# Threshold attention with a squared-ReLU MLP on one core: the second MLP layer by Strassen's seven products, in chunks of 256 tokens

## The chip, the cores and the metric

The kernel runs on one NeuronCore of a Trainium2 chip. The metric is the device time of one execution, in microseconds (us); the time of a kernel is the median of its runs. Engines are called as in the profile: PE (TensorE; PEld is its weight loading), DVE (VectorE), ACT (ScalarE), POOL (GpSimd), SP (SyncE, whose queue issues nearly all DMAs here).

## The reference

All arrays are float32 (the weights come from the host as 8-byte words, which the kernel reads as double precision and rounds itself).

```python
# q, k, v: (8, 8, 576, 64)   w_in: (512, 2048)   w_out: (2048, 512)
scores = q @ k.T / sqrt(64)
thresh = max(scores, -1) - tau            # tau = 0.02
scores = where(scores >= thresh, scores, -1e9)
attn = exp(scores - max(scores, -1)); attn /= attn.sum(-1) + 1e-9
x = (attn @ v)                            # to (8 * 576, 512): tokens x heads * dims
out = relu(x @ w_in) ** 2 @ w_out         # (4608, 512)
```

## The kernel before

**Attention.** Heads are taken in pairs, four pairs (`HP`) to a batch element, 32 pairs in all. A *visit* is a pair with a list of query blocks, and a *step* is one block of 128 queries (the fifth block, of 64 queries, takes both heads in one tile). There are 160 steps. In a step:

- `scores` (L168): PE computes q k^T of both heads into two PSUM tiles `s0`, `s1` (2 banks each, one copy); DVE takes the maxima (L186) and the thresholds (L187).
- `exponents` (L191): ACT computes exp (L196) into `w`.
- `threshold` (L199): DVE compares the scores with the threshold, multiplies and sums (L208). Only then are the score tiles free for the next step.
- `divide` (L215): POOL multiplies by the reciprocal sums (L220).
- The weights are then transposed to `wT`. The first eleven visits do this on PE two steps later (`turn`, L223, through PSUM and ACT); from step 35 on (`by_dma`) DVE transposes blocks of 32 (`turn_blocks`, L258, one step later) and SP's DMAs place them (`place_blocks`, 16 or 8 DMAs).
- `mix` (L281): PE multiplies by v (L291), ACT copies the result into `xT`, the MLP's input with the channels on the partitions (L295 to L300).

`load_qk`, `load_v` and `prep` (L155) bring in q, k, v of the next visit; `prep` transposes q and k on DVE (L160) into `qT`, `kT`, two buffers of each.

**Weights.** 32 pieces of 128 x 512 (16 of `w_in`, 16 of `w_out`) are loaded by DMA four pieces ahead and rounded by `round_weights` (L101): ACT twice, DVE three times (L116 to L119), POOL twice (L121, L123), in two buffers shared with `turn_blocks`. They are spread over the first 34 steps.

**MLP.** Tokens go in 12 chunks of 384. `mlp_in` (L306): for each of 16 blocks of 128 hidden units, 4 matmuls of 384 columns into `h`; ACT applies ReLU (L317), POOL squares (L318) into `g`. `mlp_out` (L322): for each 128 tokens, 16 matmuls of 512 columns with `g` as the stationary operand, into `o`; ACT copies `o` out (L332) and SP stores it.

**Order.** The order on every engine is written out by the loop at the end; nothing is reordered afterwards. Four times a step `fill` takes matmul pieces of the MLP from a list (`waiting`) and puts them between attention's work. `rate` says how many microseconds' worth a step gets, so that the list lasts until the next chunk's tokens are complete (`chunk_at`). The first four pairs are visited twice, first with three blocks and then with two, so that chunk 0 is complete in step 14; chunk 1 follows in step 40. Until weights are rounded (`out_from`), only the first layer of chunk 0 is spread. After the last step everything left is emitted at once.

Of the kernel before, what the change touches and what calls it, by code (L numbers as in the profile page):

```python
# [19 lines left out]
def kernel(  # L20
# [14 lines left out]
    P = 128  # L35
# [7 lines left out]
    TCH = 384  # L43
    NCH = n_tokens // TCH
    SCALE = 0.125
    assert (H % 2, D, REST, NBLK, d_model) == (0, 64, 64, 4, H * D)
    assert n_tokens == B * S and (2 * S) % TCH == 0 and SCALE * SCALE * D == 1.0
# [13 lines left out]
    w_out_sb = const.tile([P, NFT, d_model], FP32, name="w_out_sb")  # L61
# [5 lines left out]
    qmid = [const.tile([P, P], FP32, name=f"qmid{i}") for i in range(2)]  # L67
    for i in range(2):
        nc.gpsimd.memset(vs[i], 0.0)
        nc.gpsimd.memset(qmid[i], 0.0)  # L70

    WP = 512
    n_in = d_ff // WP * NMC
    n_pieces = n_in + NFT * d_model // WP
    area = {}

    def weight_piece(i):

        if i < n_in:
            f, c = divmod(i, NMC)
            cols = slice(f * WP, (f + 1) * WP)
            return moe_w_in[c * P:(c + 1) * P, cols], w_in_sb[:, c, cols]
        i -= n_in
        return moe_w_out[i * P:(i + 1) * P, :], w_out_sb[:, i, :]

    RAW = 4

    def weight_area(i):  # L90
        if not area:
            area["a"] = pool.tile([P, NMC, 2 * S], FP32, tag="xT", name="area").rearrange("p c s -> p (c s)")
        at = (i % RAW) * 2 * WP
        return area["a"][:, at:at + 2 * WP]

    def load_weights(i):
        nc.sync.dma_start(out=weight_area(i).bitcast(mybir.dt.int64), in_=weight_piece(i)[0])

    rounding = {}

    def round_weights(i, stage):  # L101
# [6 lines left out]
        if stage == 0:  # L108
            rounding[i] = pool.tile([P, 3, WP], FP32, tag="wb", name="cv")
        t, e, d = (rounding[i][:, x, :] for x in range(3))  # L110
# [9 lines left out]
        elif stage == 2:  # L120
            nc.gpsimd.tensor_tensor(out=d, in0=d, in1=e, op=ALU.mult)  # L121
        else:
            nc.gpsimd.tensor_tensor(out=weight_piece(i)[1], in0=t, in1=d, op=ALU.add)  # L123

    loaded, ready = {}, {}

    def load_qk(n):
# [4 lines left out]
        tiles = []  # L132
        for name, t in (("ql", q), ("kl", k)):
            x = pool.tile([P, S // 32, 32], FP32, tag=name, name=name)
            for m in range(4):
# [3 lines left out]
                nc.sync.dma_start(out=to[:, last:, :], in_=src[:, 0:S // 32 - last, :])  # L139
                if last:  # L140
                    nc.sync.dma_start(out=to[:, 0:last, :], in_=src[:, S // 32 - last:, :])
            tiles.append(x)
        loaded[n] = tiles
# [11 lines left out]
    def prep(n, part):  # L155

        if part == 0:
            ready[n] = [pool.tile([P, S], FP32, tag="qT", name="qT"), pool.tile([P, S], FP32, tag="kT", name="kT")]
        qT, kT = ready[n]
        nc.vector.transpose((qT, kT)[part], loaded[n][part].rearrange("p c d -> p (c d)"))  # L160
        if part == 0 and NBLK in visits[n][1]:
            for u in range(2):
                rows = slice(u * D, (u + 1) * D)
                nc.gpsimd.tensor_copy(out=qmid[n % 2][rows, u * D:(u + 1) * D], in_=qT[rows, NBLK * P:S])
# [3 lines left out]
    def scores(vis, i):  # L168

        qT, kT = ready[vis]  # L170
# [5 lines left out]
        for half, u in halves:  # L176
            if i < NBLK:
                rows, lhsT = slice(u * D, (u + 1) * D), qT[u * D:(u + 1) * D, i * P:(i + 1) * P]
            else:
                rows, lhsT = slice(0, P), qmid[vis % 2]  # L180
# [7 lines left out]
        w = pool.tile([P, n, S], FP32, tag="w", name="w", bufs=3)  # L188
# [33 lines left out]

    def turn(vis, i, part):  # L223

        w = weights[vis, i][0]
        ps = psum.tile([P, 4, P], FP32, tag="mm" if early() and part == 1 else "tx", name="w_ps", bufs=2)
# [19 lines left out]
    KB = S // 32  # L246
    blocks = {}

    def turn_blocks(vis, i):
# [4 lines left out]
        if not two or i % 2 == 0:  # L254
            blocks[vis, i // 2] = pool.tile([P, 2 * KB, 2, 32] if two else [P, KB, 1, 32], FP32, tag="wb", name="wb")
# [22 lines left out]
    xTs = {}  # L278
    xTs = {}

    def mix(n, cols):  # L281

        b, pr = divmod(visits[n][0], HP)
        if b // 2 not in xTs:
            xTs[b // 2] = pool.tile([P, NMC, 2 * S], FP32, tag="xT", name="xT")
        nq = cols.stop - cols.start
        ps = psum.tile([P, TCH], FP32, tag="tx", name="x_ps", bufs=2)
# [241 lines left out]
```

## Time and profile before

| | |
|---|---|
| median of 3 runs | 1491.63 us (1490.35 to 1493.38) |
| the profiled execution: time, span | 1489.97 us, 1488.2 us |
| mean granted clock of TensorE | 0.987 |
| PE, PEld busy | 1434.4 us (96%), 765.9 us (51%) |
| DVE, POOL, ACT busy | 801.2 us (54%), 527.2 us (35%), 443.6 us (30%) |
| second layer `o` (L328), first layer `h` (L313) on the chain that ended last | 34%, 32% |
| `s` (L181), `x_ps` (L291) on it | 12%, 10% |

How to read the profile's lines below. A line of groups gives source line, engine, operation, output <- inputs by the program's names, shapes, x count, then busy us and the mean ns of one, then idle time of the engine ahead of it and what ended it (`<-`). A timeline line gives start us, length us, engine, line, operation, and x how many were merged; in brackets the idle time ahead. A line of waits reads "engine line <- what it waited for: us in total, times, longest". A line of a stretch gives `from:to length`, then each engine's busy time with its instructions, then the granted clock, the DMA share and GB/s. A matmul's own length includes its way through the array; in a run of matmuls the spacing of starts is what each costs.

### The profile page before, as it was taken

The numbers are of one execution on the slowest core, as the hardware profiler recorded it, in microseconds if no ns is written. First come the engines' busy times: TensorE is split into PE (matmuls) and PEld (weight loads), VectorE is DVE, ScalarE is ACT, GpSimd is POOL, SyncE is SP. The second block draws the span as 40 slices with busy tenths as digits, with TensorE's granted clock in tenths as the row PEclk, the third lists the DMA queues.
The fourth block names the chain that finished last, engine by engine and source line by source line (L and its number), as shares of the span: only waits on it lengthen the run. The fifth ranks groups of instructions, "written<-read, shape, count | busy, mean of one in ns | idle before, by whom it ended". The sixth has DMA issues, their size and how long they took to land.

```text
span 1488.2 us, 18872 instructions
## 1 busy us (share of the span) xinstructions
PE 1434.4 (96%) x5876; PEld 765.9 (51%) x5876; DVE 801.2 (54%) x1738; ACT 443.6 (30%) x956; POOL 527.2 (35%) x779
## 2 busy tenths in 40 slices
PE   4888889999999999999999999999999999999998
PEld 3665555554455455455455455455455455455453
DVE  5888996655555555555555555555555555510000
ACT  3665564232132232232232122232232222211010
POOL 3567775243143143243233234234134134121020
PEclk9889999999999999999999999999999999999999
DMA  6456530344454554544445544544455444430000
GB/s 150 98 131 136 123 98 22 68 87 86 92 94 83 106 97 80 98 90 82 90 95 92 103 89 81 92 93 84 89 106 92 87 93 86 84 63 7 15 0 22
DMA packets 532547, 125.74 MB, mean 84 GB/s; under 512 B 523744, under 2 KB 523744, under 8 KB 532448
## 3 DMA queue, kind: packets, MB, share of 16 engines
q1 hardware_dynamic: 532416, 124.53, 43.7%
q8 instruction: 48, 0.79, 0.2%
q14 instruction: 51, 0.42, 0.1%
q0 software_dynamic: 32, 0.00, 0.0%
HBM read 48.63 MB, written 9.44 MB: 39 GB/s over the span
## 4 chain that ended last, share of the span: by engine, by line
PE 89%; DVE 7%; SPq 1%; issue 1%; POOL 1%; ACT 0%; DMA 0%; DVEq 0%; ACTq 0%
PE o L328 34%; PE h L313 32%; PE s L181 12%; PE x_ps L291 10%; DVE st L186 2%; DVE cv L117 1%; DVE w L208 1%; PE w_ps L231 1%; SPq L139 1%; DVE cv L116 1%; DVE cv L119 0%; DVE st L187 0%; DVE kT L160 0%; POOL w_out_sb L123 0%; DVE st L210 0%
## 5 line engine op out<-in xcount | busy, mean ns | idle before, releaser
L313 PE MATMUL h<-xT,w_in_sb 128*128 128x384 f32 x1536 | 517.6, 491 | 0.0
L328 PE MATMUL o<-w_out_sb,g 128*128 128x512 f32 x1152 | 513.0, 597 | 0.0
L186 DVE TENSOR_REDUCE st<-s 128x1 f32<-128x576 f32 x288 | 206.7, 752 | 382.8 <-PE s L181 382.8
L313 PEld LDWEIGHTS h<-xT,w_in_sb 128*128 128x128 f32 x1536 | 286.3, 190 | 204.1 <-issue 24.1
L328 PEld LDWEIGHTS o<-w_out_sb,g 128*128 128x128 f32 x1152 | 214.1, 190 | 260.4 <-issue 253.0
L318 POOL TENSOR_TENSOR g<-g 128x384 f32<-128x384 f32 x192 | 158.9, 828 | 352.8 <-ACT g L317 329.2
L208 DVE SCALAR_TENSOR_TENSOR w<-s,st,w 128x576 f32<-128x576 f32 x288 | 222.8, 807 | 84.4 <-ACT w L196 84.4
L220 POOL TENSOR_SCALAR w<-w,st 128x576 f32<-128x576 f32 x288 | 234.8, 824 | 34.8 <-DVE st L211 26.2
L181 PE MATMUL s<-kT,qT 64*128 64x288 f32 x1024 | 176.2, 441 | 38.4 <-DVE w L208 29.7
L196 ACT ACTIVATE w<-s,st 128x576 f32<-128x576 f32 x288 | 199.2, 737 | 12.7 <-POOL w_in_sb L123 0.4
L218 POOL TENSOR_SCALAR st<-st 128x2 f32<-128x2 f32 (+1 forms) x160 | 35.8, 224 | 469.9 <-DVE w L208 465.0
L317 ACT ACTIVATE g<-h 128x384 f32<-128x384 f32 x192 | 94.1, 490 | 328.5 <-PE h L313 328.5
L291 PE MATMUL x_ps<-wT,vs 128*64 128x128 f32 (+3 forms) x1700 | 181.7, 363 | 9.8 <-ACT wT L232 8.4
L258 DVE STREAM_TRANSPOSE wb<-w 128x576 f32<-128x576 f32 x225 | 162.8, 757 | 14.1 <-DMA wT<-wb 7.4
L181 PEld LDWEIGHTS s<-kT,qT 64*128 64x128 f32 x1024 | 99.0, 191 | 133.5 <-issue 79.5
L291 PEld LDWEIGHTS x_ps<-wT,vs 128*64 128x64 f32 x1700 | 108.1, 144 | 83.1 <-issue 16.7
L295 ACT COPY xT<-x_ps 128x256 f32<-128x256 f32 x50 | 18.6, 372 | 245.9 <-PE x_ps L291 245.9
L194 ACT ACTIVATE st<-st 128x2 f32<-128x2 f32 (+1 forms) x160 | 32.7, 205 | 181.2 <-DVE st L186 180.4
L332 ACT COPY osb<-o 128x512 f32<-128x512 f32 x36 | 21.1, 585 | 168.7 <-PE o L328 168.7
L121 POOL TENSOR_TENSOR cv<-cv 128x512 f32<-128x512 f32 x32 | 40.8, 1274 | 56.3 <-DVE cv L119 52.5
L232 ACT COPY wT<-w_ps 128x384 f32<-128x384 f32 x84 | 38.3, 482 | 60.4 <-PE w_ps L231 60.2
L187 DVE TENSOR_SCALAR st<-st,ntau 128x2 f32<-128x2 f32 (+1 forms) x160 | 44.6, 279 | 5.7
(36 smaller groups left out, 480.2 us busy)
## 6 DMA issues: line engine op xcount, KB each, us to landing
wT<-wb SPq DMA_DIRECT2D x800, 72.0 KB, 2.2
ql<-in_q_dram SPq DMA_DIRECT2D x144, 72.0 KB, 2.7
vs<-in_v_dram SPq DMA_DIRECT2D x72, 128.0 KB, 2.7
out_dram<-osb SPq DMA_DIRECT2D x36, 256.0 KB, 2.2
area<-in_moe_w_in_dram SPq DMA_DIRECT2D x16, 512.0 KB, 4.2
area<-in_moe_w_out_dram SPq DMA_DIRECT2D x16, 512.0 KB, 3.7
kl<-in_k_dram SPq DMA_DIRECT2D x72, 72.0 KB, 2.8
kl<-in_k_dram SPq DMA_DIRECT2D x72, 64.0 KB, 2.4
```

The costliest lines, as they stand in the source:

```text
L181: nc.tensor.matmul(sc[u][:, half, 0:HALF], lhsT, kT[rows, half * HALF:(half + 1) * HALF], start=True, stop=True)
L186: nc.vector.tensor_reduce(out=mx[:, u:u + 1], in_=sc[u][:, :, 0:HALF], axis=AX.XY, op=ALU.max)
L187: nc.vector.tensor_scalar(out=thr, in0=mx, scalar1=ntau8, scalar2=None, op0=ALU.add)
L196: nc.scalar.activation(out=w[:, u, :].rearrange("p (h k) -> p h k", h=2), in_=sc[u][:, :, 0:HALF], func=AF.Exp, bias=bias[:, u:u + 1], sca ...
L208: nc.vector.scalar_tensor_tensor(out=wu, in0=sc[u][:, :, 0:HALF], scalar=thr[:, u:u + 1], in1=wu, op0=ALU.is_ge, op1=ALU.mult, accum_out=s ...
L220: nc.gpsimd.tensor_scalar(out=w[:, u, :], in0=w[:, u, :], scalar1=z[:, u:u + 1], scalar2=rcp[:, u:u + 1], op0=ALU.add, op1=ALU.mult)
L258: nc.vector.transpose(wb[:, u * KB:(u + 1) * KB, i % 2, :], w[:, u, :].rearrange("p (k q) -> p k q", q=32))
L291: nc.tensor.matmul(ps[u * D:(u + 1) * D, 0:nq], vs[n % 2][:, u * (NBLK + 1) + c, :], wT[:, cw, cols], start=(c == 0), stop=(c == NBLK))
L313: nc.tensor.matmul(h, w_in_sb[:, c, f * P:(f + 1) * P], xT[:, c, at:at + TCH], start=(c == 0), stop=(c == NMC - 1))
L317: nc.scalar.activation(out=g, in_=h, func=AF.Relu)
L318: nc.gpsimd.tensor_tensor(out=g, in0=g, in1=g, op=ALU.mult)
L328: nc.tensor.matmul(o, gs[j, f][:, t * P:(t + 1) * P], w_out_sb[:, f, :], start=(f == 0), stop=(f == NFT - 1))
```

## The change

The second layer is computed by Strassen's scheme in the chunks from the third on (`j >= PLAIN`, `PLAIN = 2`). A chunk has 256 tokens, two halves A and B of 128; `w_out` is cut into four quarters of 1024 x 256 (`Q00`, `Q01`, `Q10`, `Q11`), and `g` into `g0` and `g1` (hidden units 0 to 1023, and the rest). Seven products of a 128 x 1024 with a 1024 x 256 matrix, each 8 matmuls of 256 columns, replace the eight that the plain layer amounts to (16 matmuls of 512 columns for each half). They need

- sums and differences of quarters of the weights (`FT1` to `FT4`), made once on DVE by `sum_quarters`, 16 instructions of 512 columns in the first layer of chunk 2;
- sums of `g` in `gsum`: two on POOL for each half of the hidden blocks (`square_half`, four instructions of 512 columns a chunk), and two differences on DVE, in two instructions each, that overwrite them between the products;
- seven DVE additions of 256 columns a chunk that read the products from PSUM, with one ACT copy of the first product. They write `osb`; the ACT copies of `o` go, except in the two plain chunks.

Around this:

- Chunks have 256 tokens (`TCH`), so `mlp_in` has 256 columns and there are 18 chunks. ReLU and squaring go over two hidden blocks at once (512 columns). A piece of PE work is 4 matmuls of 256 columns (or 2 of 512), and the follow-up work of a piece on ACT, POOL, DVE and SP is emitted after the next piece instead of at once (`state["then"]`).
- The first four pairs' visits have two and then three blocks (`FIRST = 2`). A piece waits in the list until the weights it needs are rounded (`state["rounded"]`), and the list's rate until step 35 covers both layers of chunk 0.
- Fewer buffers for attention: one `qT`, `kT`, `qmid`; rows of q and k in two buffers for the first visits and one later; two `w` from step 35 on; `xT` is a ring of six chunks; weight pieces are loaded three ahead and rounded in three buffers; `g` is one buffer of a chunk. The room of `FT1`, `FT2`, `FT4` holds loads and buffers of the beginning.
- `prep` of the next visit follows the maxima in a visit's last step, ahead of `threshold`, and that step's rounding on DVE and POOL comes behind `threshold`; from step 35 on `prep` comes behind `threshold`. k of the first visit is loaded by ACT's queue.
- PSUM: banks 4 and 5 for `turn` and `mix` (4 alone from step 35 on); banks 6 and 7 for the plain chunks; banks 5, 6, 7 in rotation for `h` and the products of the others.

The core of the diff:

```diff
-    TCH = 384
+    TCH = 2 * P
...
-    def mlp_in(j, f, part):
-        xT, at = xTs[j * TCH // (2 * S)], j * TCH % (2 * S)
-        if part == 0:
-            hs[j] = psum.tile([P, TCH], FP32, tag="mm", name="h", bufs=2)
...
+    ring3 = [6, 5, 7]
+    def square_half(lo):
+        f = slice(lo, lo + HF // 2)
+        nc.gpsimd.tensor_tensor(out=gsum[0][:, f, :], in0=g[:, f, P:], in1=g[:, lo + HF:lo + HF + HF // 2, P:], op=ALU.add)
+        nc.gpsimd.tensor_tensor(out=gsum[1][:, f, :], in0=gsum[0][:, f, :], in1=g[:, f, 0:P], op=ALU.subtract)
+    def mlp_in(j, x):
+        f, at = FORDER[x], j * TCH % RING
+        pair = x // 2
+        if x % 2 == 0:
+            used["h"] = take("mm", (6, 7)) if j < PLAIN else bank[ring3[pair % 3]]
+        h = used["h"].rearrange("p (f n) -> p f n", f=2)
+        for c in range(NMC):
+            nc.tensor.matmul(h[:, x % 2, :], w_in_sb[:, c, f * P:(f + 1) * P], xT[:, c, at:at + TCH],
                              start=(c == 0), stop=(c == NMC - 1))
...
+        if j == PLAIN:
+            posts.append(lambda: sum_quarters(x))
+        if x % 2:
+            def square():
+                to = g[:, f - 1:f + 1, :]
+                nc.scalar.activation(out=to, in_=h, func=AF.Relu)
+                nc.gpsimd.tensor_tensor(out=to, in0=to, in1=to, op=ALU.mult)
+                if j >= PLAIN and x % 8 == 7:
+                    square_half(x // 8 * (HF // 2))
+            posts.append(square)
+        return posts
+    def sum_quarters(x):
+        which, part = divmod(x, 4)
+        f = slice(part * 2, part * 2 + 2)
+        to, a, b = ((FT1, Q01, Q00), (FT2, Q11, FT1), (FT4, FT2, Q10), (FT3, Q11, Q01))[which]
+        nc.vector.tensor_tensor(out=wo[:, to, f, :], in0=wo[:, a, f, :], in1=wo[:, b, f, :], op=ALU.subtract)
...
+    PRODUCTS = ("1", "5", "6", "2", "7", "4", "3")
+    def product(j, x, half):
...
+        left, slot, to = {
+            "1": (g0[:, :, 0:P], Q00, a), "5": (gsum[0], FT1, c), "6": (gsum[1], FT2, b), "2": (g1[:, :, 0:P], Q10, a),
+            "7": (gsum[0], FT3, b), "4": (g1[:, :, P:], FT4, a), "3": (gsum[1], Q11, c)}[p]
+        for f in range(half * HF // 2, (half + 1) * HF // 2):
+            nc.tensor.matmul(to, left[:, f, :], wo[:, slot, f, :], start=(f == 0), stop=(f == HF - 1))
...
+            if p == "1":
+                nc.scalar.copy(p1s, a)
+            elif p == "5":
+                halves(lambda f: tt(out=gsum[0][:, f, :], in0=g0[:, f, 0:P], in1=g0[:, f, P:], op=sub))
+            elif p == "6":
+                tt(out=u, in0=b, in1=p1s, op=add)
+                tt(out=osb[:, 0, HD:], in0=c, in1=u, op=add)
+                halves(lambda f: tt(out=gsum[1][:, f, :], in0=g1[:, f, 0:P], in1=gsum[1][:, f, :], op=sub))
+            elif p == "2":
+                tt(out=osb[:, 0, 0:HD], in0=a, in1=p1s, op=add)
+            elif p == "7":
+                tt(out=u, in0=b, in1=u, op=add)
+                tt(out=osb[:, 1, HD:], in0=c, in1=u, op=add)
+            elif p == "4":
+                tt(out=osb[:, 1, 0:HD], in0=u, in1=a, op=sub)
+                store_rows(j, 1, 2)
+            else:
+                tt(out=osb[:, 0, HD:], in0=c, in1=osb[:, 0, HD:], op=add)
+                store_rows(j, 0, 1)
...
     def fill(us):
         state["left"] += us
-        while waiting and state["left"] >= waiting[0][0] / 2:
-            cost, fn, *what = waiting.popleft()
-            state["left"] -= cost
-            fn(*what)
+        while waiting and state["left"] >= PIECE_US / 2 and waiting[0][0] <= state["rounded"]:
+            _, fn, *what = waiting.popleft()
+            state["left"] -= PIECE_US
+            if fn is mlp_out or what[0] <= PLAIN and what[1] == 0:
+                after()
+            then = fn(*what)
+            after()
+            state["then"] = then
...
-        if s <= min(chunk_at) - 2:
-            x = int(visits[n][1].index(i) != 1)
+        if s < HP * FIRST:
+            x = int(n > 0 and i == 0)
...
+        lay = on and last and more and not by_dma(n)
...
+            if lay:
+                prep(n + 1)
+            elif now:
                 round_weights(now[0], 1)
                 round_weights(now[0], 2)
-            if short and at == 1 and more:
-                prep(n + 1, 0)
-                prep(n + 1, 1)
...
             threshold(n, i)
+            if last and more and not lay:
+                prep(n + 1)
+            if lay and now:
+                round_weights(now[0], 1)
+                round_weights(now[0], 2)
```

258 lines of the change are left out of this document (164 added, 94 removed).

## The prediction

> **What bounds the kernel now.** I read the page's engine shares, its 40 slices and its chain first, then the busy time of each engine in three stretches.
>
> ```profile
> PE 1434.4 (96%) x5876; PEld 765.9 (51%) x5876; DVE 801.2 (54%) x1738; ACT 443.6 (30%) x956; POOL 527.2 (35%) x779
> ...
> PE   4888889999999999999999999999999999999998
> ...
> PE 89%; DVE 7%; SPq 1%; issue 1%; POOL 1%; ACT 0%; DMA 0%; DVEq 0%; ACTq 0%
> ```
> ```profile
> 0.00:8.65 8.65, 0.00 (x0) 0.00 (x0) 1.71 (x3) 1.28 (x1) 2.98 (x11) 1.00 0.52 85
> 8.65:229.46 220.81, 179.54 (x1228) 120.54 (x1228) 188.84 (x377) 128.17 (x286) 146.15 (x175) 0.91 0.53 121
> 229.46:1484.40 1254.94, 1254.90 (x4648) 645.35 (x4648) 610.61 (x1359) 313.58 (x669) 378.11 (x594) 1.00 0.42 78
> ```
>
> In the last three rows the first pair after the length is PE's busy time, then PEld, DVE, ACT, POOL, and the granted clock. From 229.46 us on PE has no gap (1254.90 of 1254.94 us) at full clock: there each microsecond taken from PE is a microsecond off the end. Before that PE waits 50 us in all, mostly for DVE in the loop "scores, maximum, exponent, threshold, next scores":
>
> ```profile
> PE s L181 <- DVE w L208: 31.3, 21, 5.6
> PE s L181 <- DVE kT L160: 8.7, 1, 8.7
> ```
>
> So I add three terms: the time at which PE becomes saturated, PE's work from there on, and the waits that the change brings into that work.
>
> **PE's price of a matmul.** Every float32 product stands as two matmul rows ("passes"): 12 chunks x 64 products give the 1536 passes of `h`. Pitches come from unbroken runs, less the last pass's own length:
>
> ```profile
> 1404.62 38.54 PE L313 MATMUL h<-xT,w_in_sb 128*128 128x384 f32 x119
> 1443.00 41.36 PE L328 MATMUL o<-w_out_sb,g 128*128 128x512 f32 x96
> ...
> 710.49 1.13 PE L181 MATMUL s<-kT,qmid 128*128 128x288 f32 x4
> ```
> ```profile
> L313 PE MATMUL h<-xT,w_in_sb 128*128 128x384 f32 x1536 | 517.6, 491 | 0.0
> L328 PE MATMUL o<-w_out_sb,g 128*128 128x512 f32 x1152 | 513.0, 597 | 0.0
> L313 PEld LDWEIGHTS h<-xT,w_in_sb 128*128 128x128 f32 x1536 | 286.3, 190 | 204.1 <-issue 24.1
> ```
>
> 384 columns: (38.54 - 0.49) / 118 = 0.3225 us. 512: (41.36 - 0.60) / 95 = 0.4291. 288: (1.13 - 0.41) / 3 = 0.240. The slope between the first two is 0.833 ns a column, with no visible fixed part, so I take 0.3225 - 128 x 0.000833 = 0.2158 us for 256 columns, which no row shows. Bounds: from below 0.213 (proportional to 384 and 512 alike, 0.833 x 256); from above the weight load. It takes 0.190 and runs beside the pass ahead of it; 0.190 is under 0.2158, but the room shrinks from 0.13 to 0.026 us. If it needed all of that and 10 ns more, the pitch were 0.226.
>
> The Trainium skill, "TensorE: Matmul & The Clock Gate", Part 3 (The mechanism), says that a weight load overlaps matmuls in flight only when it goes to another row group. These loads fill all rows, so by that rule load and pass would stand in line. The trace disagrees: 0.3225 leaves no place for a 0.190 load beside 384 columns at 0.833 ns. By the rule the sum below would grow by 3968 x 0.19 = 754 us; I keep the row.
>
> Chunks of 256: `h` 16 x 4 x 2 = 128 passes; seven products of 8 matmuls, 2 passes each, 112 more: 240 x 0.2158 = 51.8 us. Before, 256 tokens cost two thirds of 128 x 0.3225 + 96 x 0.4291 = 82.5, that is 55.0. Gain 3.2 us x 16 chunks = 51 us. The two plain chunks cost 128 x 0.2158 + 64 x 0.4291 = 55.1 each: nothing.
>
> **Where saturation starts.** With two blocks in the first four visits, chunk 0 is complete in step 10 instead of 14 and chunk 1 in step 21; the third chunk comes in step 40 as before. Following the planner (pieces wait for rounded weights), chunk 0's pieces go out at about 1.3 a step (2.3 us, as before) and all but one are done when step 35 begins; from there 33 plain pieces and then Strassen chunks are queued without a pause that matters. Before, chunk 0's second layer still stood entirely ahead at 229.46, the start of step 32. These rows give the steps' length:
>
> ```profile
> 8.65 2.30 PE L181 MATMUL s<-kT,qT 64*128 64x288 f32 x8 [8.65 <-DVE kT L160]
> ...
> 173.45 1.24 PE L181 MATMUL s<-kT,qT 64*128 64x288 f32 x8 [0.45 <-DVE w L208]
> 179.97 2.40 PE L291 MATMUL x_ps<-wT,vs 128*64 128x128 f32 x20 [4.47 <-ACT wT L232]
> 186.33 1.00 PE L181 MATMUL s<-kT,qT 64*128 64x288 f32 x6
> ...
> 229.46 1.97 PE L181 MATMUL s<-kT,qT 64*128 64x288 f32 x8 [0.57 <-DVE w L208]
> ...
> 255.89 1.24 PE L181 MATMUL s<-kT,qT 64*128 64x288 f32 x8
> ```
> ```profile
> ACT cv L113 <- POOL w_out_sb L123: 8.6, 2, 4.9
> ```
> ```profile
> L160 DVE STREAM_TRANSPOSE qT<-ql 128x576 f32<-128x576 f32 x36 | 27.9, 776 | 1.2 <-DMA ql<-in_q_dram 0.9
> L117 DVE SCALAR_TENSOR_TENSOR cv<-cv 128x512 uint32<-128x512 uint32 x32 | 31.3, 977 | 3.5 <-ACT cv L113 0.3
> L121 POOL TENSOR_TENSOR cv<-cv 128x512 f32<-128x512 f32 x32 | 40.8, 1274 | 56.3 <-DVE cv L119 52.5
> L208 DVE SCALAR_TENSOR_TENSOR w<-s,st,w 128x576 f32<-128x576 f32 x288 | 222.8, 807 | 84.4 <-ACT w L196 84.4
> L332 ACT COPY osb<-o 128x512 f32<-128x512 f32 x36 | 21.1, 585 | 168.7 <-PE o L328 168.7
> L295 ACT COPY xT<-x_ps 128x256 f32<-128x256 f32 x50 | 18.6, 372 | 245.9 <-PE x_ps L291 245.9
> ```
>
> 32 steps took 229.46 - 8.65 = 220.8, 6.90 each; 35 steps end at 8.65 + 241.5 = 250.2. Corrections: k of visit 0 goes by ACT's queue beside q's, so the 8.7 us wait shortens, but ACT has its one instruction of 1.28 us there (first of the three stretches): -1 (0 to -2). Three rounding buffers instead of two: the ACT wait for POOL (8.6 us in 2) that made the step from 173.45 to 186.33 almost 13 us long: -5 (0 to -8.6). In the last steps of seven visits (the four of three blocks, the three long ones after them) the rounding's DVE work moves behind the threshold, where of its roughly 2 us the next scores (1.24) cover an estimated 1.1 (-1.1 each); one set of qT and kT puts two transposes (about 1.5) back into the loop in three of them: -3 (+5 to -8). Loading three pieces ahead instead of four: a step is longer than a landing; 0. Saturation from 241; ends 228 and 262.
>
> **Work from there on.** Attention's part of PE after step 35, from before's steps 35 on:
>
> ```profile
> 256.00:1484.50 1228.50, 470.42 (x1408) 263.60 (x1408) 1.00 0.43 80
> ...
> 256.00:1484.50 1228.50, 496.60 (x1116) 207.74 (x1116) 1.00 0.43 80
> ```
>
> (`h`, then `o`, alone): 1228.5 - 1408 x 0.3225 - 1116 x 0.4291 = 295.5. The new MLP work: 16 x 8 x 0.2158 + 17 x 4 x 0.4291 + 480 pieces x 8 x 0.2158 = 27.6 + 29.2 + 828.7 = 885.5. Together 1181; PE ends at 241 + 1181 = 1422 without new waits.
>
> **New waits.** Seven additions a chunk of 256 columns out of PSUM (0.36 to 0.5 us; nearest row L208, 576 columns, 0.807) and four of 512 in SBUF (like L117: median 0.693, longest 1.58, mean 0.977; I take the mean) put 7 us a chunk on DVE, 16 more such for the sums of weights: 801 + 129 = 930 us, 65%. POOL gets 4 x 1.274 a chunk (L121), 527 + 82 = 609 us in all, 42%; ACT loses most of L332. None becomes the bound by its sum. What can cost is DVE's order: an addition put between the transposes and the threshold delays the next scores. The tightest step is a visit's second one (601.39 below):
>
> ```profile
> L117 DVE SCALAR_TENSOR_TENSOR cv<-cv x32: 691/693/1582, 14.2 to 241.9; 128x512 uint32<-128x512 uint32 x32
> ```
> ```profile
> wT<-wb SPq DMA_DIRECT2D x800, 72.0 KB, 2.2
> ```
> ```profile
> 601.39 1.24 PE L181 MATMUL s<-kT,qT 64*128 64x288 f32 x8
> ...
> 604.52 1.44 DVE L258 STREAM_TRANSPOSE wb<-w 128x576 f32<-128x576 f32 x2 [0.17 <-DMA wT<-wb]
> 605.89 0.78 DVE L208 SCALAR_TENSOR_TENSOR w<-s,st,w 128x576 f32<-128x576 f32 x1
> 606.59 0.81 DVE L208 SCALAR_TENSOR_TENSOR w<-s,st,w 128x576 f32<-128x576 f32 x1
> ...
> 607.91 0.51 PE L181 MATMUL s<-kT,qT 64*128 64x288 f32 x2
> ...
> 701.61 10.45 SPq L269 DMA_DIRECT2D wT<-wb  x16
> ...
> 707.54 0.81 DVE L208 SCALAR_TENSOR_TENSOR w<-s,st,w 128x576 f32<-128x576 f32 x1
> ...
> 719.59 0.65 PE L291 MATMUL x_ps<-wT,vs 128*64 128x256 f32 x4
> ...
> 1484.44 0.59 ACT L332 COPY osb<-o 128x512 f32<-128x512 f32 x1 [13.15 <-PE o L328]
> ```
>
> The threshold ends 0.5 us ahead of the next scores, with DVE busy until it starts. A fourth step has 710.49 - 708.35 = 2.1 us. Three new pieces (5.2 us) fill such a step as three old ones did. Following the planner, seven steps have more additions in their first quarter than room; the excess is 7 us in all with the mean for the SBUF additions, 4.4 with the median, 13 with the longest. The Trainium skill, "SBUF — State Buffer", Who interferes with whom, has a DVE instruction with two SBUF inputs wait for a POOL instruction that reads SBUF, whole; the trace agrees as far as L117's 693 to 1582 ns go, and by a full wait for L121 behind each addition the excess would be about 18 us. Elsewhere: list empty in steps 79 and 159, so `h` waits for a mix's copy (L295, 0.37, and about as much around it, twice: 1.4); plain chunk 1 waits for its last ReLU and the next chunk for two L332 copies (2); product operands from POOL and DVE, which have a product or more (3.45 us) of cover (2; up to 32 if the cover goes). SP's stores wait for DVE instead of ACT, 34 instead of 36; wT's moves queue behind them, and the mix waits for those. The last of the sixteen issued from 701.61 lands at 701.61 + 10.45 + 2.2 = 714.3, the mix that reads them starts at 719.59: 5 us to spare, so 0. Sum 12, ends 5 and 45.
>
> The tail of 3.8 us (span 1488.2) loses 0.2. Span 1422 + 12 + 3.6 = 1437.6; the profiled execution took 1489.97 against its span of 1488.2, so +1.8; it lay 1.7 under the median of 1491.63, so I say 1441.
>
> **The rivals.** (1) Slower: the weight load shows through at 256 columns, in `h` and the products. For it: only 26 ns of room. Against: 288 columns, 58 ns of room, show nothing. It decides at 1491.6 - 1441 = 51 us over 3968 passes, 13 ns, a pitch of 0.229; at 0.24 the time is 1441 + 96 = 1537. The skill's rule quoted above is its extreme, 1441 + 754 = 2195 us; with the 384-column run against it I give that less than one of this rival's 6 in 100. (2) DVE and POOL come late in ordinary steps: a quarter of a microsecond in each of 125 steps gives 1441 + 31 = 1472. For: 0.5 us margins. Against: the fourth steps' 2.1 us. (3) The beginning gains nothing and the added matmuls delay it: saturation at 262, 1441 + 21 = 1462. For: PE was 81% busy there. Against: as many microseconds a step are put in as before. (4) The products wait for the sums and the seven cost as much as eight: 16 x 3.2 = 51, 1492, no change.
>
> **How the numbers follow.** Forecast 72% (its own range 1426 to 1458), rival 1 6%, 2 11%, 3 8%, 4 3%. The range of 1419 to 1480 holds the forecast, 2 and 3. A kernel of this length can be told from no change by 0.2%, 3 us. Faster: forecast, 2, 3, less a share in which they add up: 0.89; same 0.03; slower 0.08.
>
> **What would show it.** Right: `h` and product rows at a pitch of 0.216 in the tail, 2304 and 1792 passes; PE without gaps from 235 to 250 us on; PE's waits for DVE after that under 15 us; DVE near 65%. Wrong: a weight-load idle share gone and a pitch over 0.22; scores waiting for L208's successor in most steps; product rows waiting for POOL's or DVE's sums; saturation after 260.

## The result, and the profile after

The changed kernel takes 1451.14 us (median; 1450.02 to 1453.96), the kernel before 1492.3 us in the same comparison: ratio 0.9728, 95% interval 0.9711 to 0.9746. That is 41 us faster; 1441 was forecast, with a range of 1419 to 1480. The profiled execution took 1450.02 us, its span is 1448.2.

From the page: TensorE's and the other engines' shares, TensorE's 40 slices and the chain by engine.

```profile
PE 1387.1 (96%) x7412; PEld 1058.0 (73%) x7412; DVE 904.5 (62%) x1930; ACT 423.1 (29%) x904; POOL 623.9 (43%) x794
...
PE   5898888999999999999999999999999999999998
...
PE 65%; SPq 20%; DVE 6%; issue 3%; DMA 2%; ACT 2%; POOL 1%; DVEq 0%; ACTq 0%; POOLq 0%
```

TensorE lost 47 us of work (1434.4 to 1387.1) and is still 96% busy. New is SP's queue: 20% of the chain where it was 1%. By stretches, cut at the start of step 35 and the last matmul (busy of PE, PEld, DVE, ACT, POOL, then the clock); the last two rows are the same stretch of before and its score groups, ahead of which stand the score groups of after:

```profile
0.00:240.31 240.31, 197.83 (x1395) 135.41 (x1396) 199.47 (x415) 136.86 (x301) 159.20 (x193) 0.95 0.51 115
240.31:1444.60 1204.29, 1189.22 (x6018) 922.61 (x6017) 704.58 (x1514) 286.29 (x603) 464.72 (x602) 1.00 0.44 81
```
```profile
240.31:1444.60 1204.29, 155.43 (x900) 91.36 (x900) 1.00 0.44 81
```
```profile
255.86:1484.40 1228.54, 1228.50 (x4506) 631.00 (x4505) 594.56 (x1323) 302.12 (x644) 363.47 (x574) 1.00 0.43 80
```
```profile
255.86:1484.40 1228.54, 152.46 (x900) 88.04 (x900) 1.00 0.43 80
```

Before, TensorE stood still for 0.04 us in this stretch; now for 1204.29 - 1189.22 = 15.1 us, and the 900 score passes take 3.0 us longer, which are waits too (a group of eight that starts before the threshold has freed its second tile stretches over the wait). The visible ones, TensorE's waits behind 240 us:

```profile
PE bank L318 <- DMA wT<-turned: 3.5, 4, 1.7
PE bank L430 <- DVE osb L449: 2.9, 2, 1.9
PE bank L430 <- DVE u_sum L445: 1.6, 1, 1.6
PE bank L398 <- POOL wo L144: 1.5, 1, 1.5
PE s L199 <- DVE kT L178: 1.4, 3, 0.6
PE bank L430 <- DVE osb L452: 1.2, 3, 0.5
PE bank L367 <- ACT osb L405: 1.2, 1, 1.2
PE bank L318 <- issue: 1.1, 2, 0.8
PE s L199 <- DVE w L227: 0.5, 1, 0.5
```

L318 is the mix (4.6 us), L430 a product that waits until VectorE has emptied the PSUM bank it is to write (5.7 us). The groups that carry the sum, and an unbroken run of first-layer passes and one of products at the end:

```profile
L367 PE MATMUL bank<-xT,w_in_sb 128*128 128x256 f32 x2304 | 519.8, 382 | 3.5 <-POOL w_in_sb L144 2.4
...
L239 POOL TENSOR_SCALAR w<-w,st 128x576 f32<-128x576 f32 x269 | 236.4, 888 | 31.2 <-DVE st L230 25.2
...
L430 PE MATMUL bank<-wo,gsum 128*128 128x256 f32 x1024 | 234.2, 382 | 2.9 <-DVE u_sum L445 1.6
...
L430 PE MATMUL bank<-wo,g 128*128 128x256 f32 x768 | 178.7, 383 | 2.9 <-DVE osb L449 2.9
...
L443 DVE TENSOR_TENSOR gsum<-g 128x512 f32<-128x512 f32 x32 | 20.8, 681 | 107.3 <-PE bank L430 107.3
```
```profile
1371.91 7.07 PE L430 MATMUL bank<-wo,gsum 128*128 128x256 f32 x32
...
1392.63 27.79 PE L367 MATMUL bank<-xT,w_in_sb 128*128 128x256 f32 x128
```

(27.79 - 0.38) / 127 = 0.2158 us and (7.07 - 0.38) / 31 = 0.2158: the forecast pitch to its last digit, with 2304 and 768 + 1024 = 1792 passes.

What took the place of the forecast's "5 us to spare" is SP's queue in one visit (start, length, line, transfers):

```profile
598.51 2.21 SPq L161 DMA_DIRECT2D ql<-in_q_dram  x4
600.77 1.58 SPq L161 DMA_DIRECT2D kl<-in_k_dram  x3
...
603.99 22.46 SPq L299 DMA_DIRECT2D wT<-turned  x32
626.54 0.55 SPq L411 DMA_DIRECT2D out_dram<-osb  x1
...
629.48 10.35 SPq L306 DMA_DIRECT2D wT<-turned  x16
639.92 0.54 SPq L411 DMA_DIRECT2D out_dram<-osb  x1
640.50 2.12 SPq L161 DMA_DIRECT2D ql<-in_q_dram  x4
```

The next visit's first load is issued at 640.50, 41.99 us after this one's, and the pauses between the rows are 0.11 us at most: 48 issues of turned blocks (three times sixteen; "16 or 8 DMAs" above is wrong, none has eight; 32.8 us), 10 loads of q and k (5.2), 4 of v (2.1) and two stores (1.1), 41.2 us in all. The queue is full, and TensorE is all but full beside it: from the start of step 35 to that of step 155, which is 24 visits, a visit takes 41.7 us on average and TensorE is busy for 986.7 of 1001.4 us.

The trace of before already showed a queue that was nearly full, with the same issues in visits of 42.3 us. Its waits for blocks that VectorE hadn't turned yet, before and after (L269 of the kernel before is L299 here):

```profile
SPq L269 <- DVE wb L258: 48.5, 23, 14.6
```
```profile
SPq L299 <- DVE turned L288: 24.6, 6, 15.3
```

Apart from the longest wait, that was 1.5 us a visit in 22 visits, and 9.3 us in five waits is left. So the queue had some 1.5 us a visit to spare, and the shorter visits used most of it.

### The profile page after: what moved, and what is told of

Its sections match the earlier page's. It is cut to its first block, busy times and chain, and to the rows that moved or that the text cites. A ratio compares the mean times of both kernels' runs of the same rounds, so it can differ in the third digit from the quotient of the medians.

```text
span 1448.2 us, 22131 instructions
## 1 busy us (share of the span) xinstructions
PE 1387.1 (96%) x7412; PEld 1058.0 (73%) x7412; DVE 904.5 (62%) x1930; ACT 423.1 (29%) x904; POOL 623.9 (43%) x794
## 4 chain that ended last, share of the span: by engine, by line
PE 65%; SPq 20%; DVE 6%; issue 3%; DMA 2%; ACT 2%; POOL 1%; DVEq 0%; ACTq 0%; POOLq 0%
PE bank L367 26%; PE bank L430 16%; SPq L299 12%; PE s L199 9%; PE bank L318 8%; SPq L306 5%; PE bank L398 3%; SPq L161 3%; DVE st L204 2%; PE bank L257 1%; SPq L163 1%; DVE w L227 1%; DVE turned L288 1%; DMA vs<-in_v_dram 1%; DVE turned L138 1%
## 5 line engine op out<-in xcount | busy, mean ns | idle before, releaser
L367 PE MATMUL bank<-xT,w_in_sb 128*128 128x256 f32 x2304 | 519.8, 382 | 3.5 <-POOL w_in_sb L144 2.4
L367 PEld LDWEIGHTS bank<-xT,w_in_sb 128*128 128x128 f32 x2304 | 431.6, 190 | 84.2 <-issue 21.3
L378 POOL TENSOR_TENSOR g<-g 128x512 f32<-128x512 f32 x144 | 149.8, 1042 | 232.2 <-ACT g L377 209.4
L430 PE MATMUL bank<-wo,gsum 128*128 128x256 f32 x1024 | 234.2, 382 | 2.9 <-DVE u_sum L445 1.6
L430 PEld LDWEIGHTS bank<-wo,gsum 128*128 128x128 f32 x1024 | 192.5, 190 | 38.6 <-issue 7.6
L199 PE MATMUL s<-kT,qT 64*128 64x288 f32 x1024 | 176.8, 438 | 30.4 <-DVE kT L178 10.3
L318 PE MATMUL bank<-wT,vs 128*64 128x128 f32 (+3 forms) x1700 | 179.7, 358 | 8.7 <-DMA wT<-turned 3.5
L430 PE MATMUL bank<-wo,g 128*128 128x256 f32 x768 | 178.7, 383 | 2.9 <-DVE osb L449 2.9
L288 DVE STREAM_TRANSPOSE turned<-w 128x576 f32<-128x576 f32 x225 | 163.0, 758 | 10.1 <-DMA wT<-turned 3.8
L430 PEld LDWEIGHTS bank<-wo,g 128*128 128x128 f32 x768 | 143.8, 190 | 32.4 <-issue 8.2
L318 PEld LDWEIGHTS bank<-wT,vs 128*64 128x64 f32 x1700 | 107.9, 141 | 78.1 <-issue 25.6
L398 PE MATMUL bank<-wo,g 128*128 128x512 f32 x128 | 62.0, 619 | 7.3 <-POOL wo L144 7.0
```

Of the source, the lines that this page charges most:

```text
L199: nc.tensor.matmul(sc[u][:, half, 0:HALF], lhsT, kT[rows, half * HALF:(half + 1) * HALF], start=True, stop=True)
L288: nc.vector.transpose(wb[:, u * KB:(u + 1) * KB, i % 2, :], w[:, u, :].rearrange("p (k q) -> p k q", q=32))
L318: nc.tensor.matmul(ps[u * D:(u + 1) * D, 0:nq], vs[n % 2][:, u * (NBLK + 1) + c, :], wT[:, cw, cols], start=(c == 0), stop=(c == NBLK))
L367: nc.tensor.matmul(h[:, x % 2, :], w_in_sb[:, c, f * P:(f + 1) * P], xT[:, c, at:at + TCH], start=(c == 0), stop=(c == NMC - 1))
L378: nc.gpsimd.tensor_tensor(out=to, in0=to, in1=to, op=ALU.mult)
L398: nc.tensor.matmul(o[t].rearrange("p (h d) -> p h d", h=2), g[:, f, t * P:(t + 1) * P], mov, start=(f == 0), stop=(f == NFT - 1))
```

## The experiments

The open question is the 11 us between the forecast's 1193 us behind 240 (1181 of work, 12 of waits) and the 1204.3 measured. Theory SYNC blames SP's queue, theory VECTOR the order on VectorE. Times are medians; ratios are against the kernel before, beside which each ran.

**The yardstick** is the changed kernel again.

> The changed kernel itself once more, as the yardstick for the other kernels of this call: 1451 us by both theories. Both theories start from the same gap: from the start of step 35 at 240.3 us the matmuls of the changed kernel add up to 1181 us, as forecast, but the stretch lasted 1204 us, so that about 23 us are waits of TensorE where 12 were forecast. Theory SYNC: SyncE's issues of turned weight blocks fill the queue nearly without a pause (48 of 0.65 us with 10 loads of queries and keys, 4 of values and some 2 stores make about 40 us of a visit of 42), so blocks land late and mixes wait. Theory VECTOR: VectorE's new differences and additions, put between the transposes and the threshold of the next block, make scores and the operands of products late.

1450.86 us, ratio 0.9731 (0.9715 to 0.9748). Its profiled execution has 12.8 us of idle TensorE in the same stretch and 156.3 us of scores. The differences below are to this one; two kernels of it are told apart from about 2.5 us on.

**SP's loads given to ScalarE's queue.**

```diff
-            elif not short and at == 1 and more:
+            elif not short and at == 1 and more and not by_dma(n):
...
+                load_v(n + 1, act=by_dma(n))
+            if by_dma(n) and more and at in (1, 2):
+                load_qk(n + 1, which=(at - 1,), act=True)
```

> In the visits whose weights are turned by transfers, the loads of the next pair's queries, keys and values are issued from ScalarE's queue at the end of a step (queries in step 1, keys in step 2, values in the last step) and no longer by SyncE. SyncE has about 14 x 0.5 = 7 us of each visit of 42 back. SYNC: the waits for turned blocks (3.5 us listed at the mixes, and the mixes and scores that come late behind them) shrink; 8 to 12 us less, 1439 to 1443. VECTOR: nothing that VectorE does is moved; within 2 us of 1451, or up to 3 slower by ScalarE's issues.

1636.53 us, ratio 1.0978 (1.0955 to 1.1001): 186 us slower, which neither theory had. SP's waits behind 240 us in this kernel:

```profile
SPq L300 <- DMA vs<-in_v_dram: 194.9, 25, 12.3
SPq L300 <- DMA ql<-in_q_dram: 150.0, 23, 8.8
```

A block's transfer (L300 here) has no use for these loads, and yet by these rows it waited 345 us for their landing, once for each in nearly every visit; the yardstick has no such row. Issued by ScalarE, the loads stand behind exponents that wait for VectorE (442.9 us of such waits, 313.0 in the yardstick), which would hold SP up too. Why the two are tied together the runs don't show. The experiment says nothing on SYNC.

**The loads left out**, SYNC's test without a second queue:

```diff
     def load_qk(n):
+        if n > 3 * HP + 1:
+            return
...
     def load_v(n):
+        if n > 3 * HP + 1:
+            return
```

> Leaves out the loads of queries, keys and values from pair 14's visit on (the tiles keep the values of an earlier pair, and every instruction that reads them stays), so that SyncE issues 14 transfers, about 7 us, less in each visit of 42 us, and nothing waits for a queue. SYNC: the waits at mixes and the scores that come late behind turned blocks go; of the 12.7 us in which TensorE stood still behind 240 us and the 4 us by which score groups ran long in the yardstick run, 5 to 10 us less, 1441 to 1446. VECTOR: at most 2 us less, 1449 to 1451, since VectorE's instructions all stay.

1446.07 us, ratio 0.9697 (0.9684 to 0.9711): 4.8 us less, a little short of SYNC's 5 to 10. The evidence is on SP's side. Its waits for blocks that VectorE hasn't turned yet, in the yardstick and in this kernel (L299 and L303 are the same line):

```profile
SPq L299 <- DVE turned L288: 23.1, 7, 14.8
```
```profile
SPq L303 <- DVE turned L292: 194.9, 48, 15.6
```

In the yardstick SP was hardly ever ready first; here it has some 170 us to spare, 7.8 us for each of the 22 visits without loads. No wait of a mix is left in TensorE's list. The median from a block's issue to its landing is 2.2 us with the loads and without, which speaks for the queue, though the loads' traffic has gone as well.

**VectorE's differences left out.**

```diff
-                halves(lambda f: tt(out=gsum[0][:, f, :], in0=g0[:, f, 0:P], in1=g0[:, f, P:], op=sub))
+                pass
...
-                halves(lambda f: tt(out=gsum[1][:, f, :], in0=g1[:, f, 0:P], in1=gsum[1][:, f, :], op=sub))
```

> Leaves out VectorE's four differences behind products 5 and 6 of each Strassen chunk (two of 681 ns and two of 734 ns by the trace after; the products then read sums where differences belong). 16 x 2.83 = 45 us of VectorE's 705 behind 240 us go, TensorE's passes all stay. VECTOR: banks of products are emptied sooner and thresholds come on time: 5.7 us listed at products for VectorE and 3.7 us of long score groups shrink by half or more, 4 to 9 us less, 1442 to 1447. SYNC: within 2 us of 1451.

1451.27 us, ratio 0.9737 (0.9724 to 0.9751): nothing, with 42 us less on VectorE. VECTOR alone falls. But look at where waits went: the scores take 153.2 us behind 240 (156.3 in the yardstick), 3.1 us less, and the mixes wait more (yardstick, then this kernel):

```profile
PE bank L318 <- DMA wT<-turned: 1.4, 1, 1.4
...
PE bank L318 <- issue: 1.0, 3, 0.5
```
```profile
PE bank L318 <- DMA wT<-turned: 5.2, 4, 2.3
...
PE bank L318 <- issue: 1.5, 2, 1.2
```

That is 6.7 us against 2.4. The first execution of the changed kernel, above, had 4.6, so some 2 us of the difference are scatter between executions.

**Both left out.** That reading can be tested: if what VectorE saves ends at SP's queue, it must come through once the queue has room.

> Leaves out both the loads of queries, keys and values from pair 14's visit on and VectorE's four differences of each Strassen chunk. Alone, the first gave 4.8 us and the second nothing, though without the differences the score groups fell by 3.3 us; the mixes and their waits for turned blocks grew by about as much. Theory in series (VectorE's share of the waits is covered by SyncE's queue: what VectorE saves ends at turned blocks that aren't placed yet): without the loads the 3 us come through, 1441 to 1443.5. Rival (the differences lie beside other work and cost nothing under any load of SyncE): the time without the loads, 1445 to 1447.

1440.38 us, ratio 0.9651 (0.9638 to 0.9664): 10.5 us under the yardstick and 5.7 under the kernel without loads, where the differences alone gave nothing. The two lie in series, as the first theory said, and the time is a little below its range. The size of the second step is less sure than its sign: the two profiled executions (1442.18 and 1443.41 us) are the slowest of the one kernel and the fastest of the other and lie only 1.2 us apart. In the traces the stretch from step 35 to the last matmul takes 1203.5 us in the yardstick, 1205.1 without the differences, 1197.5 without the loads and 1195.2 without both.

**Follow-up work held until behind the threshold.**

```diff
-        fill(quarter)
+        fill(quarter, keep=on and by_dma(n))
...
             threshold(n, i)
+            release()
```

> The work that follows a piece (relu, square, quarter sums, additions of products), where it would be emitted in the first quarter of a step that turns its weights by transfers, is emitted only behind that step's threshold, so that VectorE goes from the blockwise transposes straight to the threshold. VECTOR: scores are ready sooner and the hidden waits in the score groups (about 8 us over the steps whose scores last 1.94 us where 1.24 is usual) go; 6 to 10 us less, 1441 to 1445. SYNC: within 2 us of 1451, or slower by a few us where a bank is freed later for the next piece.

1461.67 us, ratio 0.9802 (0.9785 to 0.9818): 10.8 us slower, against VECTOR, and more than the few us that SYNC allowed for a bank freed late. The scores did get their 2.5 us (153.8), but the products pay, by TensorE's waits behind 240 us:

```profile
PE bank L430 <- DVE osb L452: 8.3, 6, 2.4
PE bank L430 <- DVE osb L449: 4.7, 4, 2.1
PE bank L430 <- DVE u_sum L445: 3.5, 2, 1.9
```

16.5 us where there were 5.7. With three banks in rotation, an addition that is late by one threshold stops the next product; holding is the wrong way round.

**No Strassen.** All else stays.

```diff
-    PLAIN = 2
+    PLAIN = NCH
```

> All 18 chunks of 256 tokens take the plain second layer, none the seven products; the chunk size, the early part and the buffers stay as changed. A chunk has 64 plain passes of 512 columns instead of 112 of 256: 64 x 0.429 = 27.5 us in place of 112 x 0.216 = 24.2, so 16 chunks add 16 x 3.3 = 53 us of matmuls; the forecast's 51 comes from the same sum. Both theories: 1451 + 53 = 1504 less the waits that the products bring (6 us listed at the products by SYNC's and VECTOR's reading of the trace alike): 1490 to 1500. Under VECTOR the 16 x 15 VectorE instructions go as well and the hidden waits with them, 1482 to 1492; under SYNC the visits get longer, which leaves SyncE more room, but by 1.3 us a visit only: 1493 to 1503.

1496.69 us, ratio 1.0037 (1.0024 to 1.0050): within the range of both theories together (1490 to 1500) and within SYNC's, but above VECTOR's 1482 to 1492. The products are worth 45.8 us: TensorE's work falls by 1440.3 - 1387.1 = 53.2 (50.1 against the yardstick's 1390.2) and waits take 4 to 7 back. Without them visits last 43.0 us, SP waits 56.6 us for blocks, and no mix waits: the queue has room again, as SYNC says. And without them the change is 6 us slower than the kernel before. Its stretch, and what TensorE waits for in it:

```profile
242.50:1490.90 1248.40, 1238.50 (x5251) 769.89 (x5249) 600.02 (x1323) 297.86 (x618) 365.78 (x538) 1.00 0.43 78
```
```profile
PE bank L367 <- ACT osb L405: 5.5, 5, 1.8
PE bank L398 <- ACT g L377: 2.7, 3, 0.9
```

9.9 us of idle TensorE where before had none: 8.2 at the seams of chunks, of which there are 18 instead of 12 (the forecast's "plain chunk" waits, many times), and 1.6 for the last rounded weights. TensorE is also busy for 10.0 us more than in the stretch of before (1238.50 against 1228.50), 4.1 of which before had done ahead of step 35. The two eat the 13.4 us by which step 35 starts sooner (242.50 against 255.86) and 6.5 more. The fewer buffers, which came with the smaller chunks, aren't separated from them.

**The early part as before**, the rest as changed.

```diff
-    FIRST = TCH // P
+    FIRST = 3
...
-            x = int(n > 0 and i == 0)
+            x = int(i != 1)
```

> The early part as before the change: the first visits of each of the first four pairs take three blocks of queries and the second two, with the old rule for which step rounds a piece of the weights; chunks, products and buffers stay as changed. The first chunk is complete some steps later and TensorE has no chunk to fill its pauses with until then. In the trace of before TensorE stood still for 41.1 us ahead of step 35, in the changed kernel for 31.7. If that difference is the order of the early part: 1451 + 9 = 1460 (1456 to 1464). If it came from the smaller chunk alone, which has 256 tokens to complete and not 384: within 3 us of 1451.

1461.18 us, ratio 0.9797 (0.9783 to 0.9810): 10.3 us slower, so the early order is worth that. It isn't all standing still, as the expectation had it: TensorE is idle for 47.6 us ahead of step 35 and for 42.5 in the kernel after, and its busy time in all grew from 1387.1 to 1395.7 us. (By the same stretches, less the start, the expectation's 41.1 and 31.7 are 41.3 and 33.5.) Step 35 and what follows, by the stretches:

```profile
259.64:1458.00 1198.36, 1183.64 (x5982) 921.02 (x5981) 704.47 (x1514) 283.92 (x599) 460.10 (x597) 1.00 0.44 81
```

That is 19.3 us later than 240.31, and the stretch behind it is only 5.9 us shorter, by matmuls already done. The forecast's third rival, the beginning that gains nothing, was priced at saturation 262 and 1462 us. If the worths add up, the 10.3 us here and the 6 us that the kernel without products loses make some 16 us, an estimate of what small chunks and fewer buffers cost.

**A margin for the weights.**

```diff
-        while waiting and state["left"] >= PIECE_US / 2 and waiting[0][0] <= state["rounded"]:
+        while waiting and state["left"] >= PIECE_US / 2 and waiting[0][0] <= state["rounded"] - (state["rounded"] < n_pieces):
```

> Until all weights are rounded, a piece of a chunk is let into TensorE's order only when one more piece of the weights is rounded than it reads, so that no piece stands ahead of scores while its weights are still being rounded. Early theory (waits that TensorE spends on late weights in the first 240 us, 7.0 us at the plain second layer and 2.4 at the first, come out of the end of the early part): saturation 3 to 5 us sooner, 1446 to 1448. Rival (the early part is paced by the chain from threshold to threshold, and what TensorE doesn't wait for here it waits for elsewhere): within 2 us of 1451.

1459.56 us, ratio 0.9787 (0.9774 to 0.9800): 8.7 us slower; both theories missed. Step 35 starts at 245.76. Until then TensorE waits 1.8 us for POOL's weights (7.8 in the kernel after), but longer for VectorE (36.9 us, with kT's 8.9, against 30.0):

```profile
PE s L199 <- DVE w L227: 18.0, 12, 3.5
PE s L199 <- DVE wo L227: 10.0, 7, 3.3
```

A piece that waits for its weights waits, it seems, in time in which scores would wait for the threshold anyway. Step 35 starts 5.2 us later than in the yardstick (240.56), and what follows takes 3.1 us more (1206.6 against 1203.5), which this run doesn't explain. The rival had the first part's mechanism, and not that it costs.

**One plain chunk less**, in two versions.

```diff
-    PLAIN = 2
+    PLAIN = 1
```

> The second chunk also takes the seven products, so that one chunk is left with the plain second layer; the quarter sums are made behind that chunk's first-layer pieces, which the trace shows to run wholly behind 240 us, when all weights are rounded. 64 passes of 512 columns at 0.429 us become 112 of 256 at 0.216: 27.5 - 24.2 = 3.3 us less matmul work, 1447.6, less or more by the waits: the 16 quarter sums (16 x 0.67 = 10.7 us of VectorE) then lie just behind the rounding. SYNC: 1447 to 1449. VECTOR: 1448 to 1452, since VectorE has 0.67 us more behind each piece of that chunk at the time when it has just caught up.

1456.94 us, ratio 0.9771 (0.9756 to 0.9785). By the code, the sums here overwrite the third weight buffer while attention still reads it, which changes the output, and each waits for the other; little follows. The second version also has:

```diff
-            used["h"] = take("mm", (6, 7)) if j < PLAIN else bank[ring3[pair % 3]]
+            used["h"] = take("mm", (6, 7)) if j <= PLAIN else bank[ring3[pair % 3]]
...
-        if j == PLAIN:
-            posts.append(lambda: sum_quarters(x))
+        if j == PLAIN and x >= NFT // 2:
+            posts += [lambda y=y: sum_quarters(2 * x - NFT + y) for y in range(2)]
```

> The second chunk takes the seven products too, but its quarter sums follow its later first-layer pieces, two behind each of the last eight, when attention no longer uses the third weight buffer, which lies in the same memory, and its first layer keeps to the two banks that the turning of weights doesn't use. The matmul work falls by 27.5 - 24.2 = 3.3 us: 1447 to 1449 if TensorE's work sets the time there. Rival: VectorE gets 16 x 0.67 = 10.7 us of sums in about 14 us, beside attention, and gives the 3 us back as waits: 1450 to 1453.

1458.91 us, ratio 0.9776 (0.9761 to 0.9792): 8 us slower where 3.3 less work was at stake. Two waits grew most:

```profile
PE bank L318 <- DMA wT<-turned: 5.9, 8, 1.2
PE s L199 <- DVE w L227: 5.3, 4, 3.5
```

The scores wait 4.8 us more than in the yardstick: the sums stand ahead of thresholds. The mixes wait 4.5 us more, and step 35 starts 2.2 us later (242.75), part of which may be scatter: it starts at 240.2 without the differences and at 241.7 without both, where the early part is the yardstick's. Together, less the 3.3 us, that is 8.2; the medians differ by 8.1, and the spans of the two profiled executions by 10.0.

**What a weight load costs.** The first rival, measured by itself: the same columns in passes of half the length, with a load for each.

```diff
-        for c in range(NMC):
-            nc.tensor.matmul(h[:, x % 2, :], w_in_sb[:, c, f * P:(f + 1) * P], xT[:, c, at:at + TCH],
-                             start=(c == 0), stop=(c == NMC - 1))
+        for y, c in ((y, c) for y in (0, P) for c in range(NMC)):
+            nc.tensor.matmul(h[:, x % 2, y:y + P], w_in_sb[:, c, f * P:(f + 1) * P],
+                             xT[:, c, at + y:at + y + P], start=(c == 0), stop=(c == NMC - 1))
```

> Each first-layer matmul of 256 columns becomes two of 128 with the same weights loaded for each, everything else as changed: 4608 passes of 128 columns instead of 2304 of 256, the same columns in all. Bounds by rows: streaming alone, half of 0.216 = 0.108 us a pass, no change of the time (about 1451 to 1465 with the switches); weight loads of 0.190 us, hidden behind a pass of 0.216 but not behind one of 0.108, as the pace: 2176 x (2 x 0.190 - 0.216) = 357 us more, about 1808. Load and pass one after the other, 0.190 + 0.108 = 0.298: 2176 x (0.596 - 0.216) = 827 more, about 2280. The forecast's first rival, by which loads show through at 256 columns already, puts the pace near the second or third of these.

1470.25 us in one execution. Its loads, and an unbroken run near its end:

```profile
L367 PEld LDWEIGHTS bank<-xT,w_in_sb 128*128 128x128 f32 x4608 | 526.1, 193 | 28.0 <-issue 21.3
```
```profile
1411.94 28.75 PE L367 MATMUL bank<-xT,w_in_sb 128*128 128x128 f32 x256
```

(28.75 - 0.28) / 255 = 0.1116 us a pass, 0.004 over half of 0.2158. The loads' mean of 193 ns is no pace: 4608 x 0.193 = 889 us lie within 526 us of busy time, so the rows of loads overlap one another. Whether two loads run at once or a load is shorter than its row, the trace doesn't tell. At 256 columns the room is at least 0.1 us and not the 0.026 that the forecast counted. The time is 19 us up. Behind step 35 the stretch is 14.5 us longer than in the yardstick (1218.0 against 1203.5), about the 4352 passes x 0.0037 = 16; the rest lies ahead of step 35, which starts 6.3 us later, and isn't explained by its 256 passes.

## Why the prediction was right, and where its sizes were off

| | forecast | measured |
|---|---|---|
| saturation (step 35) | 241 us | 240.3 |
| pitch of 256 columns | 0.2158 us | 0.2158 |
| TensorE's work from there | 1181 us | 1189.2 busy, 3 of it waits in score groups |
| new waits, as idle time | 12 us | 15.1 |
| tail | 3.6 us | 3.6 |
| execution against span; median against execution | +1.8; +1.7 | +1.8; +1.1 |
| VectorE, POOL busy | 930, 609 us | 904.5, 623.9 |

**Right.** Three quarters of the work is pitch times passes, and the pitch holds to the last digit; the experiment without products gives their worth as 45.8 us, of a gain of 51. Saturation was right as a total but not in each part, so its hitting within 1 us is partly luck. The wait for POOL in the rounding is gone, as forecast (8.6 us before, no such row after). But k by ScalarE's queue was to bring the first scores 1 us sooner, and they start at 8.97 us instead of 8.65; and TensorE waits 7.8 us for rounded weights there, which the sum hadn't.

**Mis-sized: "New waits", 12 us.** The measured excess over 1181 is 23.3 us: 15.1 idle, 3.0 in score groups, and 5 of matmul time. Of the 5, 3.6 fit more and shorter runs: the three MLP lines are 922.8 us busy, 37.3 over passes times pitch, where before the two were 33.7 over. By parts:

- Scores: 7 forecast, 3.5 measured (3.0 hidden, 0.5 visible).
- Empty list: 1.4 forecast, none visible.
- Plain chunks: 2 forecast, 1.2 measured (L367). Not forecast: 1.5 us for the last rounded weights (L398) and 1.4 for `kT`, which has one buffer now.
- "Product operands": 2 forecast. Operands were never late; the banks were, 5.7 us. The forecast priced what a product reads and not where it writes.
- SP and the mixes: 0 forecast, 4.6 measured (2.4 in the yardstick). This is the term that was wrongly put at nothing: "5 us to spare" was read from one transfer of one visit. The spare time belongs to the queue, which had some 1.5 us a visit left before, and none in the visit of 42.0 us above with its 41.2 us of issues. The three experiments with loads and differences put SP and VectorE together at 10.5 us by the medians and 8.3 by the stretches, most of the missing 11.

**The rivals.** (1) A load that shows through: refuted, with more room than the forecast had given it. (2) VectorE late in ordinary steps: the mechanism is there, but it hides behind SP; the differences alone came to 5.7 us where SP had room, of the 31 priced. (3) The beginning: refuted by saturation at 240.3; right as a price, since undoing that part gives 1461 against 1462. (4) Waiting products: 5.7 us, a ninth of what decides.

**Slips in its working.** The room at 288 columns is 0.240 - 0.190 = 50 ns, not 58. The corrections to the saturation add up to ends of 231.6 and 255.2 us, not 228 and 262. Neither moves the forecast.

**Weight loads, and VectorE beside POOL.** The Trainium skill, "TensorE: Matmul & The Clock Gate", Part 2 (LDWEIGHTS), puts a load at its columns divided by 1.2 in ns, which makes an estimate of 107 ns for 128 columns. The trace agrees as far as a pass of 0.1116 us with a load of its own leaves room for that; the 190 ns of the load rows are no pace. By the rule that the prediction quotes from the Trainium skill, Part 3 (The mechanism) of the same page, load and pass would stand in line; the measured pitch at 256 columns, which is that of the columns alone, refutes it once more. The Trainium skill, "SBUF — State Buffer", Who interferes with whom, has a VectorE instruction with two inputs in SBUF contend with a POOL instruction that reads SBUF. The trace agrees that they do, but here it is POOL that pays: its division takes 824 ns before, 888 after, and in the kernel without VectorE's differences 841:

```profile
L239 POOL TENSOR_SCALAR w<-w,st 128x576 f32<-128x576 f32 x269 | 224.0, 841 | 31.4 <-DVE st L230 25.2 <-POOL st L237 0.9
```

so that 47 of the 64 ns come from these. VectorE hardly paid: its differences took 681 and 734 ns where the forecast put 977.

## What to carry to other kernels

When a kernel is bound by one engine, the sum of passes times pitch gives the gain; then add up each issuing queue over a period as if it were an engine, in the trace of before already, because a queue that is full turns any hurry elsewhere into waiting. Where an edit gives nothing, look whether its gain comes back at the next wait, and try it again with that one relieved: 0 and 4.8 us alone were 10.5 together. Smaller pieces fill gaps sooner, but each seam can cost: here 18 chunks for 12, together with fewer buffers, used up more than the earlier start had gained, and only the products paid for it.

None of the complete versions beats the changed kernel. What the runs point to is fewer issues by SP in a visit (the last block's sixteen take 10.35 us for 16 or 20 KB each); that wasn't tried.

## What the runs showed of the hardware that was not expected

- Rows of weight loads of 128 x 128 in float32 overlap one another: listed at 193 ns each, the loads kept up with passes of 0.1116 us.
- Issuing a small strided transfer took SP's queue 0.65 to 0.70 us (16 in 10.35, 32 in 21.84 to 22.46), whether it moves 72 KB or 16 to 20, and a load of q, k or v 0.4 to 0.6; 64 issues with the stores fill a 42 us visit.
- With loads moved to a second queue, the first queue waited for their landing, 345 us over 48 waits, with nothing in the program's data that asks for it; the cause stays open.
